# The gMLP's second input half as seven block products over pairs of tiles

## The chip, the core and the metric

The kernel runs on one core of a Trainium2 chip. TensorE (PE) multiplies, VectorE (DVE) and ScalarE (ACT) work elementwise and read the products out of PSUM, GpSimd (POOL) does small and elementwise work in SBUF, and SyncE (SP) issues transfers. Each engine takes its instructions in the order of the program and waits at the first one whose operands are not ready. The metric is the device time of one execution in microseconds (us); the time of a kernel is the median of its runs.

## The reference

Two layers, each a linear attention block A followed by a gated MLP B. The change lies in the second half of `x @ w_in`, which becomes z2:

```
def _B_ref(x, w_in, w_sp, b_sp, w_out):
    z = _gelu(jnp.einsum("bsd,df->bsf", x, w_in))
    z1 = z[..., :Fh]
    z2 = _layernorm(z[..., Fh:], axis=-1)
    g = jnp.einsum("ts,bsf->btf", w_sp, z2) + b_sp[None, :, None]
    return jnp.einsum("bsf,fd->bsd", z1 * g, w_out)

for the two layers:
    x = x + _A_ref(_layernorm(x), A_wqkv, A_wo)
    x = x + _B_ref(_layernorm(x), ...)
```

x is 2048 x 512, `w_in` 512 x 1792 (two halves of 896), `w_sp` 2048 x 2048, all float32.

## The kernel before

The 2048 rows are 16 tiles of 128. A float32 product is three matmuls (`mm3`, lines 115 to 117): both operands are split into a high part h, which ACT copies out (line 101), and a low part l, the rest, which DVE subtracts (line 104), and h·h, h·l and l·h are added up in PSUM. The order of all instructions is written by hand; nothing is reordered later. There are 8 PSUM banks and 22 pages of 128 x 512 in SBUF, handed out oldest first, 4 big tiles (`bigs`) and 6 quads.

A layer has four stages.

- **P1** (`P1.run`, 17 steps) makes keys, values and queries. A step turns a tile (DVE transpose, line 242), splits it, makes K (12 matmuls) and up to step 10 Q (12 more), and adds to the four G banks (12). At the end of a step come side pieces: a weight piece of 128 x 512 is split by ACT and DVE. Fifteen pieces (wv, wo and seven of win2, the second half of `w_in`) are spread over steps 1 to 10: one a step in the first five, two after that.
- **transition** makes the combined matrix W2.
- **P2** (`P2.run`, steps s = 1 to 18) is where the change lies. In step s DVE turns the scaled queries of tile s (`b_high`, transpose, then the high part on ACT), does the denominators of tile s+2 (`a2_den`, lines 556 to 558) and the low part (`b_low`); PE multiplies tile s-1 by W2 (`c`, 12 matmuls); DVE adds it to x (`c2`, line 597) and takes its statistics (lines 178 to 180), POOL makes rs and nb of them (lines 182 to 185), and ACT normalises (`c3`, line 191). `a2_mul` (line 565) and `a` (POOL, line 544) prepare later queries. `d_high` and `d_low` turn and split tile s-2, which came back from DRAM. `e4` normalises z of tile s-4 (ACT, 128 x 896, and for the first eight tiles a subtraction on DVE, line 663). `e` multiplies tile s-3 by win2, two banks of 448 columns with 12 matmuls each, `e2` takes GELU of the banks (line 652), `e3` the statistics of z. Then `f` runs twice: 12 matmuls of 128 x 512 for z1, four tiles at a time, a GELU on ACT (line 677) and a store. f has no work before step 6; seven calls belong to four tiles, so steps 9, 13 and 17 have one call, and five calls are left for the start of P4. The step ends with a piece of win1 (the first half of `w_in`, low part on POOL, line 109) and, from step 8, with `sums.tick`.
- **P4** multiplies by `w_sp`, itself as seven block products of 8 steps each (24 or 18 matmuls a step), gates and makes the output. `Sums` makes the four sums of blocks of `w_sp` on POOL (line 772), once, in the first layer, and keeps them in DRAM: 11 ticks lie in P2 and 21 in P4. Weights of P4 are fetched four steps ahead.

In steps 1 to 4 PE turns the queries, and in steps 2 to 5 it turns the tiles of d, so that those lie in PSUM and not in a page.

Of the kernel before, what the change touches and what calls it, by code (L numbers as in the profile page):

```python
# [10 lines left out]
F32 = mybir.dt.float32  # L11
F32R = mybir.dt.float32r
# [41 lines left out]
def mixer_kernel(ctx: ExitStack, tc: tile.TileContext, x_in, wqkv, wo_d, win1_d, win2_d, wsp_d, bsp_d, wout_d,  # L54
# [58 lines left out]
    def mm3(out, a, b, start, stop):  # L113
# [2 lines left out]
        nc.tensor.matmul(out, ah, bl, start=False, stop=False)  # L116
        nc.tensor.matmul(out, al, bh, start=False, stop=stop)  # L117

    class Weight:


# [42 lines left out]
    def w_wo():  # L164
        return Weight(bigs, [P, 4, 512], [wo_d[c * P:(c + 1) * P, :] for c in range(4)])

    def w_in1():
        return Weight(bigs, [P, NF, 4, P], [win1_d[f] for f in range(NF)])

    def w_in2():  # L170
        return Weight(bigs, [P, 4, FH], [win2_d[f] for f in range(NF)])

    def stats(x, n):

# [72 lines left out]
    class P1:  # L247
        def __init__(self, L):
            self.L = L
            self.st = 2 * L  # L250
            self.x, self.ms, self.xT, self.pk, self.kb, self.r, self.xhl = {}, {}, {}, {}, {}, {}, {}
            self.wk, self.wq, self.wv = (w_square(wqkv, 512), w_square(wqkv, 0, True), w_square(wqkv, 1024))
            self.wo, self.win2 = w_wo(), w_in2()
            self.later = deque(range(NT - DEFER, NT))
            self.turn = Turn(f"xt{L}", range(3) if L == 0 else ())
            self.G = None
            self.zacc = None
# [153 lines left out]

        def run(self):
            side = deque()
            for w in (self.wv, self.wo, self.win2):
                side.extend([w] * len(w.pieces))
            side[0].fetch()
            ND = NT - DEFER
            for s in range(1, NT + 2):
                self.loadx(s + 3)
                self.turn.load(s + 1)  # L420
                turned = 2 <= s < NT and s not in self.turn.by_pe
                if turned:
                    self.T_high(s)
                if s == 1:
                    if not self.kb:
                        self.K(0)
                    self.K(1)
                elif 2 < s <= NT:
                    self.K(s - 1)
                self.ln_a(s + 2)  # L430
                if turned:
                    self.T_low(s)
                if s <= NT:
                    self.K_phi(s - 1)
                if s <= ND:
                    self.Q(s - 1)
                if s == NT + 1:
                    self.late()
                if s <= NT:
                    self.xsplit(s - 1)  # L440
                    self.K_split(s - 1)
                if s + 1 < NT and s + 1 in self.turn.by_pe:
                    self.T(s + 1)
                self.ln_b(s + 2)
                if s <= ND:
                    self.Q_phi(s - 1)
                if s >= 2:
                    self.Gmm(s - 2)
                if s == NT + 1:
                    self.late_phi()  # L450
                for _ in range(min(len(side), 1 if s < 6 else 2)):
                    side.popleft().piece()
                for w in list(side)[:1 if s < 5 else 2]:
                    w.fetch()


    def transition(p1, p2):
# [18 lines left out]
        banks.put(zb)  # L476
        p2.a(0)
        p1.late_phi()
        p2.win1.fetch()
        p2.win1.fetch()  # L480
        p2.zeps = small.tile([P, 32], F32, name="zeps", bufs=1)
        nc.vector.tensor_reduce(p2.zeps, p2.zbc.rearrange("p (h d) -> p h d", d=16), axis=mybir.AxisListType.X,
                                op=OP.add)
# [41 lines left out]
    class P2:  # L525
        def __init__(self, p1):
            self.L = L = p1.L
            self.p1 = p1
            self.win1, self.win2 = w_in1(), p1.win2
            self.qturn, self.xturn = Turn(f"qt{L}", range(5), True), Turn(f"yt{L}", range(4))  # L530
            self.qp, self.qT, self.x, self.ms, self.xB, self.z, self.zms = {}, {}, {}, {}, {}, {}, {}
            self.fq = deque()
            self.fnext = []

        def loadx(self, i):
            if i < NT:
# [89 lines left out]
        def d_low(self, i):  # L626
            b, home, h, l = self.dpart
            low(l, b, h)
            home.put(b)
            n, k = divmod(i, 4)  # L630
            if i in self.xB:
                pages.put(self.xB.pop(i))
            if k == 3:
                self.fnext = [(n, f) for f in range(NF)]

        def e(self, i):
            n, k = divmod(i, 4)
            h, l = self.xT[n]
            s = slice(k * P, (k + 1) * P)
            w = self.win2  # L640
            self.eb = []
            for j in range(2):
                b = banks.get([P, HF])
                o = slice(j * HF, (j + 1) * HF)
                for c in range(4):
                    mm3(b, (h[:, c, s], l[:, c, s]), (w.h[:, c, o], w.l[:, c, o]), c == 0, c == 3)
                self.eb.append(b)

        def e2(self, i):
            z = ztag(i, [P, FH], f"z{self.L}")  # L650
            for j, b in enumerate(self.eb):
                nc.scalar.activation(z[:, j * HF:(j + 1) * HF], b, AF.Gelu_apprx_tanh)
                banks.put(b)

        def e3(self, i):
            self.zms[i] = stats(ztile[i], 2)
# [8 lines left out]
        def f(self):  # L665
# [1 line left out]
                return False  # L667
            n, f = self.fq.popleft()
            h, l = self.xT[n]
            w = self.win1  # L670
            b = banks.get(PAGE)
            for c in range(4):
                mm3(b, (w.h[:, f, c, :], w.l[:, f, c, :]), (h[:, c, :], l[:, c, :]), c == 0, c == 3)
            if f == NF - 1:
                quads.put(*self.xT.pop(n))
            t = pages.get(PAGE)
# [4 lines left out]
            pages.put(t)  # L681
            return True

        def run(self, sums):
            w1 = self.win1
            for s in range(1, NT + 3):
                self.loadx(s + 1)
                self.qturn.load(s + 1)
                if s in self.qturn.by_pe:
# [10 lines left out]
                    self.a2(s + 2)  # L700
                    self.p1.late_phi()
                    self.a(s + 3)
                else:
                    if s < NT:
                        self.b_high(s)
# [18 lines left out]
                    if s <= NT + 1 and not late:  # L724
                        self.d_high(s - 2)
                        self.d_low(s - 2)
                if s >= 4:
                    self.e4(s - 4)
                self.xturn.load(s - 1)
                if s >= 3:  # L730
                    self.e(s - 3)
                    self.e2(s - 3)
                    self.e3(s - 3)
                self.f()
                self.f()
                self.fq.extend(self.fnext)
                self.fnext = []
                w1.piece(True)
                w1.fetch()
                if s > 7:  # L740
                    sums.tick()
                if s >= NT + 1:
                    self.p4.fetch(s - NT - 1)
            self.e4(NT - 1)
            self.win2.free()


    class Sums:
# [2 lines left out]

        def __init__(self):
            self.s = {(m, k): dram.tile([P, 2, 512], F32, name=f"s{m}_{k}") for m in range(1, 5) for k in range(HT)}
            self.todo = deque((k, j, h) for k in range(HT) for j in range(2) for h in range(2))
            self.ahead = deque(self.todo)
            self.raw, self.made, self.done = {}, [], []

        def fetch(self):
            if self.ahead:
                k, j, h = self.ahead.popleft()  # L760
                at = ((j, k), (j, k + HT), (2 + j, k)) if h == 0 else ((2 + j, k + HT),)
                self.raw.setdefault((k, j), []).extend(load(wsp_d[n, s]) for n, s in at)

        def store(self):

            for m, k, j, t in self.made:
                nc.sync.dma_start(self.s[m, k][:, j, :], t)
            pages.put(*self.done)
            self.made, self.done = [], []

# [4 lines left out]
        def tick(self):  # L775
# [4 lines left out]
                self.fetch()  # L780
            self.fetch()
            k, j, h = self.todo.popleft()
            if h == 0:
                a21, a22, a11 = self.raw[k, j][:3]
                self.add(1, k, j, a22, a21, a22)
                self.add(3, k, j, a21, a21, a11)
                self.done = [a21]
            else:
                _, a22, a11, a12 = self.raw.pop((k, j))
                self.add(2, k, j, a11, a22, a11)  # L790
                self.add(4, k, j, a12, a11, a12)
                self.done = [a22, a11, a12]


    class P4:
# [16 lines left out]
        def fetch(self, g):  # L812
# [5 lines left out]
                n, s = {"P1": (2, k), "P2": (2, k + HT), "P4": (0, k + HT)}[p]  # L818
                nc.sync.dma_start(t, wsp_d[n:n + 2, s].rearrange("j p t -> p j t"))
            else:  # L820
                nc.sync.dma_start(t, self.sums.s[{"P6": 2, "P7": 3, "P5": 1, "P3": 4}[p], k])
            self.raw[g] = t

        def operand(self, g):
# [174 lines left out]
        def run(self, nxt):  # L999
# [1 line left out]
            self.prepare(0, 0)  # L1001
            self.fetch(2)
            while p2.f():
                pass
            p2.win1.free()
            self.prepare(1, 1)
            self.fetch(3)
            self.prepare(None, 2)
            self.gb = [bigs.get([P, NF, 512]) for _ in range(NCHK)]
            n = len(self.steps)  # L1010
            for g in range(n):
# [1 line left out]
                self.prepare(g + 2, g + 3)  # L1013
                self.mm(g)
                self.fetch(g + 4)
                if g in (1, 4, 7) or 8 <= g < 28:
                    self.sums.tick()
                if g == 3:
                    self.loadb()
# [44 lines left out]
    for L in range(2):  # L1064
# [3 lines left out]
        p2.loadx(1)  # L1068
        transition(p1, p2)
        p2.p4 = p4 = P4(p2, sums)  # L1070
        p2.run(sums)
        nxt = P1(1) if L == 0 else None
        p4.run(nxt)
        p1 = nxt
# [31 lines left out]
```

## Time and profile before

| | |
|---|---|
| median of three runs | 1394.43 us (1394.32 to 1394.86) |
| profiled execution, its time and its span | 1395.31 us, 1393.5 us |
| granted TensorE clock | 1.0 |
| P2, a step of 13 us in layer 1 (929 to 942): PE, DVE, ACT, POOL busy | 13.00, 8.45, 5.34, 3.81 us |
| the same in layer 0 (239 to 252) | 13.00, 10.96, 4.82, 7.09 us |
| DMA over the span | 162 GB/s; the highest of 40 slices 298 GB/s |
| queues in use | SP's alone; POOL issues no transfer |

Busy times of PE are modelled and overlap from one matmul to the next, so that its rate is read from the starts of its matmuls. The other engines' busy times are those of their instructions.

### The profile page before, as it was taken

The numbers are of one execution on the slowest core, as the hardware profiler recorded it, in microseconds if no ns is written. First come the engines' busy times: TensorE is split into PE (matmuls) and PEld (weight loads), VectorE is DVE, ScalarE is ACT, GpSimd is POOL, SyncE is SP. The second block draws the span as 40 slices with busy tenths as digits, with TensorE's granted clock in tenths as the row PEclk, the third lists the DMA queues.
The fourth block names the chain that finished last, engine by engine and source line by source line (L and its number), as shares of the span: only waits on it lengthen the run. The fifth ranks groups of instructions, "written<-read, shape, count | busy, mean of one in ns | idle before, by whom it ended". The sixth has DMA issues, their size and how long they took to land.

```text
span 1393.5 us, 17586 instructions
## 1 busy us (share of the span) xinstructions
PE 1387.4 (100%) x6270; PEld 1164.0 (84%) x6270; DVE 879.5 (63%) x1251; ACT 582.1 (42%) x899; POOL 416.9 (30%) x502
## 2 busy tenths in 40 slices
PE   9999999999999999999999999999999999999998
PEld 7888888888888888888888888888888888888887
DVE  6775777853755587664567767876426445776642
ACT  6674543444432234241366655444333432342410
POOL 3343344543135541431023424432100000223310
PEclk9999999999999999999999999999999999999999
DMA  5542256776679964354645314555334323544542
GB/s 176 168 131 59 90 166 218 259 226 217 215 235 295 298 228 136 121 203 159 211 129 176 111 46 121 174 176 175 104 122 142 101 96 129 168 134 156 169 143 91
DMA packets 142457, 225.70 MB, mean 162 GB/s; under 512 B 11937, under 2 KB 50593, under 8 KB 142369
## 3 DMA queue, kind: packets, MB, share of 16 engines
q1 hardware_dynamic: 142368, 224.57, 50.1%
q8 instruction: 49, 0.80, 0.3%
q14 instruction: 40, 0.32, 0.1%
HBM read 156.63 MB, written 67.90 MB: 161 GB/s over the span
## 4 chain that ended last, share of the span: by engine, by line
PE 98%; DVE 1%; DMA 0%; POOL 0%; ACT 0%; issue 0%; SPq 0%; POOLq 0%; ACTq 0%
PE bank L117 19%; PE bank L116 19%; PE bank L115 19%; PE bank L897 13%; PE bank L898 13%; PE bank L899 13%; PE bank L203 1%; PE bank L390 0%; DMA pg<-in_wsp_dram 0%; POOL pg L772 0%; ACT z_z L191 0%; DVE st L178 0%; ACT qd L101 0%; POOL rs L183 0%; DVE den L557 0%
## 5 line engine op out<-in xcount | busy, mean ns | idle before, releaser
L898 PE MATMUL bank<-qd,pg 128*128 128x512 f32 x800 | 311.4, 389 | 0.0
L897 PE MATMUL bank<-qd,pg 128*128 128x512 f32 x800 | 311.4, 389 | 0.0
L899 PE MATMUL bank<-qd,pg 128*128 128x512 f32 x800 | 311.4, 389 | 0.0
L863 DVE TENSOR_TENSOR qd<-qd,qd 128x1024 fp32r<-128x1024 f32 x112 | 157.9, 1410 | 157.2 <-ACT qd L856 154.2
L856 ACT ACTIVATE qd<-qd 128x1024 fp32r<-128x1024 f32 x112 | 118.6, 1059 | 239.1 <-DMA qd<-s 101.7
L899 PEld LDWEIGHTS bank<-qd,pg 128*128 128x128 f32 x800 | 150.2, 188 | 31.4
L897 PEld LDWEIGHTS bank<-qd,pg 128*128 128x128 f32 x800 | 150.1, 188 | 31.2
L898 PEld LDWEIGHTS bank<-qd,pg 128*128 128x128 f32 x800 | 150.2, 188 | 31.0
L919 POOL TENSOR_TENSOR bg<-bg,pg 128x512 f32<-128x512 f32 x56 | 78.9, 1413 | 320.7 <-DMA pg<-z 308.6
L117 PE MATMUL bank<-qd,pg 128*128 128x512 f32 x384 | 149.9, 390 | 0.0
L182 POOL TENSOR_SCALAR rs<-mv 128x1 f32<-128x1 f32 x96 | 38.0, 396 | 355.4 <-DVE mv L180 351.8
L191 ACT ACTIVATE pg<-pg,nb,rs 128x512 f32<-128x512 f32 x63 | 51.0, 810 | 179.0 <-POOL nb L185 172.8
L772 POOL TENSOR_TENSOR pg<-pg,pg 128x512 f32<-128x512 f32 x64 | 93.9, 1467 | 94.4 <-DMA pg<-in_wsp_dram 88.5
L115 PE MATMUL bank<-qd,pg 128*128 128x512 f32 x288 | 112.3, 390 | 0.0
L116 PE MATMUL bank<-qd,pg 128*128 128x512 f32 x288 | 112.3, 390 | 0.0
L115 PE MATMUL bank<-bg,qd 128*128 128x448 f32 x256 | 94.1, 368 | 0.0
L117 PE MATMUL bank<-bg,qd 128*128 128x448 f32 x256 | 93.6, 366 | 0.1
L116 PE MATMUL bank<-bg,qd 128*128 128x448 f32 x256 | 93.7, 366 | 0.0
L117 PE MATMUL bank<-qd,bg 128*128 128x512 f32 x224 | 87.5, 391 | 0.0
L116 PE MATMUL bank<-qd,bg 128*128 128x512 f32 x224 | 87.5, 390 | 0.0
L115 PE MATMUL bank<-qd,bg 128*128 128x512 f32 x224 | 87.3, 390 | 0.0
L116 PE MATMUL bank<-wo,qd 128*128 128x512 f32 x224 | 87.2, 389 | 0.0
(128 smaller groups left out, 2606.9 us busy)
## 6 DMA issues: line engine op xcount, KB each, us to landing
qd<-s SPq DMA_DIRECT2D x64, 512.0 KB, 3.5
qd<-in_wsp_dram SPq DMA_DIRECT2D x48, 512.0 KB, 4.2
pg<-in_wsp_dram SPq DMA_DIRECT2D x64, 256.0 KB, 5.2
s<-pg SPq DMA_DIRECT2D x64, 256.0 KB, 5.0
pg<-x SPq DMA_DIRECT2D x64, 256.0 KB, 3.1
z<-pg SPq DMA_DIRECT2D x56, 256.0 KB, 2.7
pg<-z SPq DMA_DIRECT2D x56, 256.0 KB, 3.9
x<-pg SPq DMA_DIRECT2D x48, 256.0 KB, 2.6
```

Source lines behind the costliest of these rows:

```text
L115: nc.tensor.matmul(out, ah, bh, start=start, stop=False)
L116: nc.tensor.matmul(out, ah, bl, start=False, stop=False)
L117: nc.tensor.matmul(out, al, bh, start=False, stop=stop)
L182: nc.gpsimd.tensor_scalar(rs, mv[:, 1:2], LN_EPS, None, op0=OP.add)
L191: nc.scalar.activation(y, x, AF.Identity, bias=nb, scale=rs)
L772: nc.gpsimd.tensor_tensor(t, a, b, op=OP.add)
L856: nc.scalar.activation(w[:, 0], r, AF.Copy)
L863: nc.vector.tensor_sub(w[:, 1], r, w[:, 0].bitcast(F32))
L897: m(out, h[:, o], w[:, 0, j, :], start=start, stop=False, skip_group_check=True)
L898: m(out, h[:, o], w[:, 1, j, :], start=False, stop=False, skip_group_check=True)
L899: m(out, l[:, o], w[:, 0, j, :], start=False, stop=stop, skip_group_check=True)
L919: nc.gpsimd.tensor_tensor(u, u, z1, op=OP.mult)
```

## The change

The second half of the gMLP's input is made for two tiles at once. With the two tiles' x as rows A11, A12 and A21, A22 (halves of the 512 features) and the weight as blocks Bij of 256 x 448, the four products of blocks become seven: P1 = A11·B11, P2 = A12·B21, P3 = S4·B22, P4 = A22·T4, P5 = S1·T1, P6 = S2·T2, P7 = S3·T3, with S1 = A21+A22, S2 = S1-A11, S3 = A11-A21, S4 = A12-S2. One bank X goes on adding P1, P6, P7 and P4, and is read three times on the way. Each product is 6 matmuls of 448 columns. The block sums are made on DVE at the end of d in odd steps, from step 3 on; where d lies in PSUM, ACT copies it out first (`in_sbuf`).

The parts of win2 (seven forms, h and l) and of win1 (seven pieces, h and l) are made in P1 of layer 0, stored in DRAM by SP (`flush`), and in both layers brought in by transfers that POOL issues: forms in P1 and P2, win1 part by part ahead of f. The sums of `w_sp` all move into P4. The statistics and the normalisation of z lag by a pair, and those of the last four tiles come at the start of P4.

```diff
+    def flush():
+        while stores:
+            d, part = stores.popleft()
+            nc.sync.dma_start(d, part.bitcast(F32))
...
+        def form(self, name):
+            t, h, l = (self.work[:, i, :].rearrange("p (c f) -> p c f", c=2) for i in range(3))
...
+            if name == "T1":
+                nc.vector.tensor_sub(t, B("B12"), B("B11"))
...
+            split(h, l, src)
+            stores.extend(...)
...
+    class Parts:
+        def fetch(self):
+            while self.todo and len(self.have) < self.ahead:
+                parts = [pages.get([P, 4, P], F32R) for _ in range(2)]
+                for t, d in zip(parts, self.todo.popleft()):
+                    nc.gpsimd.dma_start(t, d.rearrange("p (c f) -> p c f", c=4))
+                self.have.append(parts)
...
+        def weights_made(self, s, side, make):
+            todo = {5: ("T1",), 6: ("T2",), 7: ("T4",), 8: ("T3",), 9: ("B11", 1), 10: ("B21", 1), 11: ("B22", 1),
+                    12: (2, 3), 13: (2, 3)}.get(s, ())
...
+            for _ in range(0 if 5 <= s < 14 else min(len(side), 1 if s < 5 else 2)):
+                side.popleft().piece()
...
+        def block_sums(self):
+            a, b = (self.in_sbuf(*r) for r in self.rows)
...
+            nc.vector.tensor_add(S1, A21, A22)
+            nc.vector.tensor_sub(S2, S1, A11)
+            nc.vector.tensor_sub(S3, A11, A21)
+            nc.vector.tensor_sub(S4, A12, S2)
+            pages.put(a, b)
+            self.S = []
+            for r in (s, t):
...
+                split(h, l, r)
...
+        def e_first(self, m):
+            i = 2 * m
+            self.X, y = banks.get([P, HF]), banks.get([P, HF])
+            self.product(self.X, m, "P1", start=True)
+            self.product(y, m, "P2", start=True, stop=True)
...
+            nc.scalar.activation(z[:, self.LO], self.X, AF.Copy)
+            self.add(i, self.LO, y)
+            banks.put(y)
+            self.gelu(i, self.LO)
+
+        def e_second(self, m):
+            i, X = 2 * m, self.X
+            Z = banks.get([P, HF])
+            self.product(X, m, "P6")
+            nc.scalar.activation(ztile[i][:, self.HI], X, AF.Copy)
+            self.product(Z, m, "P5", start=True)
+            pages.put(*self.S[0])
+            self.f()
+            self.product(X, m, "P7")
+            z = ztag(i + 1, [P, FH], f"z{self.L}")
+            nc.scalar.activation(z[:, self.HI], X, AF.Copy)
+            self.add(i + 1, self.HI, Z)
+            self.gelu(i + 1, self.HI)
+            self.f()
+            self.product(X, m, "P4", stop=True)
+            nc.scalar.activation(z[:, self.LO], X, AF.Gelu_apprx_tanh)
+            banks.put(X)
+            self.product(Z, m, "P3", stop=True)
+            self.add(i, self.HI, Z)
+            banks.put(Z)
+            self.gelu(i, self.HI)
...
                     if s <= NT + 1 and not late:
                         self.d_high(s - 2)
                         self.d_low(s - 2)
-                if s >= 4:
-                    self.e4(s - 4)
+                    if s % 2:
+                        self.block_sums()
                 self.xturn.load(s - 1)
-                if s >= 3:
-                    self.e(s - 3)
-                    self.e2(s - 3)
-                    self.e3(s - 3)
-                self.f()
-                self.f()
+                m, second = divmod(s - 3, 2)
+                if s >= 3 and not second:
+                    if m >= 2:
+                        self.e4(2 * m - 4)
+                        self.e4(2 * m - 3)
+                    self.e_first(m)
+                    self.f()
+                    self.f()
+                elif s >= 3:
+                    if m >= 1:
+                        self.e3(2 * m - 2)
+                        self.e3(2 * m - 1)
+                    self.e_second(m)
                 self.fq.extend(self.fnext)
                 self.fnext = []
-                w1.piece(True)
-                w1.fetch()
-                if s > 7:
-                    sums.tick()
+                if s <= 2:
+                    self.forms.fetch(3)
+                if s >= 4:
+                    self.win1.fetch()
...
-                if g in (1, 4, 7) or 8 <= g < 28:
+                if g % 5 in (0, 2, 3) or g >= 26:
                     self.sums.tick()
```

In `Sums` a tick of the first sixteen now loads three pages, makes three sums and stores three; a tick of the last sixteen loads two (one of them a sum that was stored), makes one and stores one.

## The prediction

> **What bounds the kernel now.** I read the shares of the engines first, then the chain that ended last, then PE's own waits.
>
> ```profile
> PE 1387.4 (100%) x6270; PEld 1164.0 (84%) x6270; DVE 879.5 (63%) x1251; ACT 582.1 (42%) x899; POOL 416.9 (30%) x502
> ```
> ```profile
> PE bank L390 <- DVE pg L385: 2.3, 1, 2.3
> ```
>
> PE is the bound: it waits once, 2.3 us at the start. PE's timeline gives its rate: the start of the next matmul minus that of this one.
>
> ```profile
> 936.56 0.39 PE L116 MATMUL bank<-qd,pg 128*128 128x512 f32 x1
> 936.79 0.39 PE L117 MATMUL bank<-qd,pg 128*128 128x512 f32 x1
> 937.02 0.36 PE L115 MATMUL bank<-bg,qd 128*128 128x448 f32 x1
> 937.22 0.37 PE L116 MATMUL bank<-bg,qd 128*128 128x448 f32 x1
> ```
>
> 512 columns cost 0.227 us, 448 cost 0.203 (24 of them run from 247.30 to 252.16 in layer 0). A P2 step is c 2.72 + e 4.87 + two f 5.45 = 13.04 us, and c2 starts 13.05 us apart. What the other engines need is a matter of their order, so next come the timelines of DVE, ACT and POOL in one step of layer 1.
>
> ```profile
> 944.74 1.05 DVE L242 STREAM_TRANSPOSE pg<-pg 128x512 f32<-128x512 f32 x1
> 945.63 0.64 DVE L556 TENSOR_REDUCE den<-pg 128x32 f32<-128x512 f32 x1
> ...
> 948.70 0.69 DVE L104 TENSOR_TENSOR pg<-pg,pg 128x512 fp32r<-128x512 f32 x1 [1.82 <-ACT pg L101]
> 950.27 0.69 DVE L597 TENSOR_TENSOR pg<-pg,bank 128x512 f32<-128x512 f32 x1 [0.88 <-PE bank L117]
> 950.99 0.69 DVE L178 BATCH_NORM_STATS2 st<-pg 128x6 f32<-128x512 f32 x1
> 951.72 0.18 DVE L180 BATCH_NORM_AGGREGATE mv<-st 128x2 f32<-128x6 f32 x1
> ...
> 954.98 0.69 DVE L104 TENSOR_TENSOR qd<-pg,qd 128x512 fp32r<-128x512 f32 x1 [1.50 <-ACT qd L101]
> ```
> ```profile
> 953.61 0.82 ACT L191 ACTIVATE pg<-pg,nb,rs 128x512 f32<-128x512 f32 x1 [4.94 <-POOL nb L185]
> 954.33 0.62 ACT L101 ACTIVATE qd<-pg 128x512 fp32r<-128x512 f32 x1
> 954.85 1.12 ACT L191 ACTIVATE z_z<-z_z,nb,rs 128x896 f32<-128x896 f32 x1
> 955.88 0.52 ACT L652 ACTIVATE z_z<-bank 128x448 f32<-128x448 f32 x1
> ```
>
> From c2 (950.27) to the end of d's low part (955.67) is 5.4 us of waiting in turn: DVE, POOL (aggregate's end 951.90 to ACT's start 953.61: 1.71), ACT, DVE. Today none of it reaches PE: c and e use what was made a step earlier. PE's end to DVE's start is 0.2 us, ACT to DVE 0.04.
>
> **The change, part by part.**
>
> *PE work.* A pair of tiles takes 42 matmuls of 448 in place of 48: 6 x 0.203 = 1.22 us, 16 pairs in the two layers: -19.5 us, if PE never waits.
>
> *The new loop in P2.* PE now depends inside a step on the slow chain. P7 adds to bank X, which ACT must first have copied out, and that copy stands in ACT's queue behind c3's normalise and d's high part, which wait for c of the same step. P6 likewise waits for the copy in `e_first`, which stands behind the block sums' high parts and two e4. And `add`, after P3, is what DVE must end before it goes on to the next step's transpose. I walk one steady pair from P3's end, in us. Odd step: add at 0.2 (0.6: between 0.43 for 256 columns, L104, and 0.68 for 512, L597) to 0.8; transpose 0.9, 1.7; denominators 1.24 (L556 to L558 without contention), 2.94; low part 0.6, 3.55 (c was done at 2.9); c2 0.72, 4.27; statistics 0.91, 5.18; POOL 1.71, 6.89; normalise 0.72, 7.61; d's high part 0.62, 8.23; low part, 8.87; four block sums of 256 columns at 0.42, 10.55; the second sum pair's high part 0.52, 11.1; two e4 at 1.03, 13.17; copy 0.52, 13.7; `add`, 14.35. PE has done c, P1, P2, two f and the next c by 13.3, so P6 waits 0.5. Even step: on ACT three GELUs at 0.5 after that add, then the high part of the queries, 16.66; low part 17.3; c2 18.0; statistics 18.9; POOL 20.6; normalise 21.4; d's high part 21.9; copy 22.4; P7 at 22.6. PE, which has done P6, P5 and one f by 19.0, waits 3.6. Then P7, f, P4, P3: 1.22+2.72+1.22+1.22, end at 29.0. The loop closes on itself, so no slack gathers: a steady pair takes 29.0 us where PE's work is 24.9 and where it took 26.1 (23.4 with one f less, steps 9 and 13, for PE's missing f is off the loop).
>
> All pairs of a layer: steps (7,8) and (11,12) +2.9 each; (9,10) +5.5; (13,14) +5.2 (a little less on ACT); (15,16) -0.4 (no queries in 16); (17,18) +1.7 (no c, but P6 waits for block sums and two e4); (5,6), no f in 5 and two copies out of PSUM (0.55 each) ahead of the sums: 26.6 for 21.2, +5.4; (3,4), no f at all: P6 waits 4.7, P7 4.3, P4 0.9, less 1.2 saved, +8.5. Together +31.7, both layers **+63.4**, PE's saving included. Bounds: 35.6 if only the steps from 7 on stall; 80 if each step loses another 0.5.
>
> *Behind the waits.* PE's queue has f, P4, P3 and the next c behind P7; DVE's next transpose waits for P3, and so c2, POOL and ACT.
>
> *P1 of layer 0.* Fifteen split pieces become four and then, from step 5, forms. The timeline of DVE shows the step full:
>
> ```profile
> 64.60 0.69 DVE L311 SCALAR_TENSOR_TENSOR z_q<-bank,z_q 128x512 f32<-128x512 f32 x1 [1.16 <-ACT z_q L310]
> 65.21 1.28 DVE L104 TENSOR_TENSOR bg<-pg,bg 128x512 fp32r<-128x512 f32 x2
> 66.41 1.07 DVE L242 STREAM_TRANSPOSE pg<-pg 128x512 f32<-128x512 f32 x1
> ...
> 74.45 1.08 DVE L242 STREAM_TRANSPOSE pg<-pg 128x512 f32<-128x512 f32 x1
> ```
>
> 8.04 us from transpose to transpose, PE's step 36 x 0.227 = 8.17. The two lows (1.2) become a subtraction of 896 (1.2), ACT's high part (0.9, waiting for it) and a low part (1.2; L104 on 128x896 is 1.29): +2.1 beyond the slot, 10.1 to 10.2. Late per step: 2.05 x 4 (steps 5 to 8), 0.7 x 2 (9, 10: low 1.2 + piece 0.6), then against 24 x 0.227 = 5.44, where DVE's period was 5.3: 1.7 (11), 1.06 x 4 (12 to 15, two pieces): 15.5. The low part of a turned tile ends about 4.4 before K needs it, so **+11**; bounds 0 and 20. P1 of layer 1 loses seven pieces; PE was full there: 0.
>
> *Transfers by SP.* 14 stores of 0.46 MB and 14 of 0.26 in some ten steps of P1 (slices 4 and 5 show 59 and 90 GB/s) and as part of what DVE makes late; SP's loads for the step stand ahead of them: 0.
>
> *Transfers by POOL.* Up to four of 0.26 MB a P2 step, 1 MB in 14 us; SP and POOL together stay under 250 GB/s. POOL issued none before, so the price of an issue on POOL is bounded by its shortest and longest instruction, 0.10 (L1095) and 1.96 (L917). After an even step's z statistics POOL has 7.7 us until the next c statistics; four issues take 0.4 to 7.8: 0, hidden. Nearest in kind are the short ones. The pages they fill were given back two f before or earlier. The Trainium skill, DMA: Bandwidth & Descriptors, Latency and other measured facts, gives about 1 us to the first byte on this path; four would be 4 us by it, the sum the same; no run shows it yet.
>
> *Sums in P4.* Layer 0's P2 loses 11 ticks (POOL there was no bound). In P4 three ticks in five steps, 9 sums x 1.47 = 13.2 of 27 us on POOL, then one a step. In steps 26 to 31 weights, tick and gate are 1.57 MB in 4.08 us, 385 GB/s against 298 in the fullest slice: some 7 us late, against four steps (16 us) of fetch ahead: 0, bound 10. Late statistics of z hide under the five f left over.
>
> The sum: 1395.3 + 63.4 + 11 = 1469.7 for the profiled execution, which lies 0.9 over the median: **1469 us**.
>
> **The rivals.**
> *PE covers it all.* P5 and f behind P6, two f behind P2, are enough; the end is then 1395.3 - 19.5 - 0.9 = 1375. For it: PE waits nowhere today, DVE has 4.6 of 13 us free. Against: the walk's loop is made of measured pieces in program order. It decides below 24.9 us a pair, that is if 4 us of 29 are not there. 0.12, of which 0.01 for waits that just eat the saving up.
>
> *POOL's issues hold up the statistics.* At 2.5 us each, four take 10 in the even step's 7.7: +2.3 for 7 pairs in two layers, +32: 1501. 0.08.
>
> *PE's clock falls in the waits.* The first ten warm-up matmuls took 4.63 us, 0.46 each, twice the rate later: (0.463-0.227) x 10 = 2.4 us lost per cooling. Eight waits per layer are of 3.4 to 4.7 us: 16 x 2.4 = +38, 1507. For it: those starts; against: nothing in this trace after 2.3 us shows an idle PE. 0.08. The Trainium skill, TensorE: Matmul & The Clock Gate, The HAM clock gate, has the clock halve after an idle window of some 3.4 us that runs freely; my waits would be at its edge, and it speaks for a few of these, not for all.
>
> **How the numbers follow.** My forecast 0.72, its own range 1430 (early steps and P1 absorbed: 1394.4 + 35.6) to 1494 (P1 20, P4 10, P2 some 6 a layer more). The clock and POOL cases reach 1507, so 1430 to 1507 leaves out 1375 and the tails. A difference under 0.2% (2.8 us) can't be told from none. Faster 0.11, same 0.01, slower 0.88.
>
> **What would show it.** PE waits on ACT's copies of the bank (before P7, 3 to 4 us, 16 times; before P6), all inside P2; PE's 448-column matmuls 672 for 768; P2 pairs 29 us apart by c2; waits in P1 of layer 0 from step 7; POOL idle before the statistics. I am wrong if c2 of a pair stays under 26 us, if the waits lie on POOL or on a transfer, or if P4 waits.

## The result

The changed kernel takes 1517.9 us (median of four runs, 1517.1 to 1521.3) against 1394.4 in the same comparison: a ratio of 1.089, 95% interval 1.0871 to 1.0909. It is slower, as forecast, but by 123 us where 75 were forecast (1469), and outside the range (1430 to 1507).

The shares of the engines and the granted clock of the profiled execution after (span 1515.3 us):

```profile
PE 1420.2 (94%) x6174; PEld 1169.8 (77%) x6174; DVE 962.5 (64%) x1399; ACT 633.9 (42%) x973; POOL 483.8 (32%) x628
PEclk9999989989999999999999998999899999999999
```

PE has 96 matmuls less and its busy time is 33 us longer. The row of the granted clock (in tenths; 9, the highest digit, is 90% or more) has four eights where the kernel before has nines throughout, and the mean clock over the span is 0.967 (1.0 before). What PE waits for (total, times, longest, in us):

```profile
PE bank L828 <- ACT z_z L857: 39.3, 12, 6.5
PE bank L828 <- ACT z_z L848: 27.1, 10, 3.0
PE bank L115 <- ACT z_h L101: 6.2, 4, 2.6
PE bank L1139 <- ACT qd L1098: 4.0, 2, 2.0
```

L828 is the first matmul of a block product; L857 and L848 are ACT's copies of bank X that P7 and P6 wait for. PE's timeline at one of them, P7 in step 8 of layer 1 (start, duration, engine, line):

```profile
998.66 0.74 PE L828 MATMUL bank<-bg 128*128 128x448 f32 x1 [6.51 <-ACT z_z L857]
999.20 0.57 PE L829 MATMUL bank<-bg,bg 128*128 128x448 f32 x1
999.57 0.57 PE L830 MATMUL bank<-bg,bg 128*128 128x448 f32 x1
...
1002.52 0.39 PE L116 MATMUL bank<-qd,pg 128*128 128x512 f32 x1
1002.75 0.39 PE L117 MATMUL bank<-qd,pg 128*128 128x512 f32 x1
```

Two losses stand in these rows. PE waits 6.51 us; then its matmuls start 0.37 us apart instead of 0.20 for 448 columns (0.43 instead of 0.23 for 512), until 3.6 us later they are at full rate again. The view of windows (bounds, length, busy time of PE, PEld, DVE, ACT and POOL, granted clock, DMA) has the clock at 0.50 from the middle of the wait to that point:

```profile
995.38:1002.21 6.83, 3.55 (x9) 3.10 (x10) 4.83 (x10) 2.79 (x5) 4.02 (x9) 0.50 0.49 159
```

DVE's and ACT's timelines before it:

```profile
986.77 0.61 DVE L840 TENSOR_TENSOR z_z<-z_z,bank 128x448 f32<-128x448 f32 x1
990.86 1.09 DVE L356 STREAM_TRANSPOSE pg<-pg 128x512 f32<-128x512 f32 x1 [3.48 <-issue]
993.50 0.68 DVE L744 TENSOR_TENSOR pg<-pg,bank 128x512 f32<-128x512 f32 x1
```
```profile
996.85 0.81 ACT L305 ACTIVATE pg<-pg,nb,rs 128x512 f32<-128x512 f32 x1 [4.23 <-POOL nb L299]
997.56 0.61 ACT L101 ACTIVATE qd<-pg 128x512 fp32r<-128x512 f32 x1
998.08 0.52 ACT L857 ACTIVATE z_z<-bank 128x448 f32<-128x448 f32 x1
```

This is the walk of the forecast, link by link: transpose, c2 (L744), statistics, POOL's nb, normalise (L305), d's high part, and only then the copy for P7. One link was not in it: the transpose starts 3.48 us late, waiting for nothing that the view names.

PE's starts split the time (work: matmuls at the full rate; cold: what slower starts add; waits: the rest; 2.2 us of the first stage after and 4.2 of the last are in none of the three):

```
                 before            after                        longer by
                 length   length   work   cold  waits
P1, layer 0       147.8    164.2   142.5   6.9   12.6              16.4
P2, layer 0       203.9    247.0   193.0  16.6   37.3              43.1
P4, P1 layer 1    486.3    498.3   486.2   4.1    8.1              12.0
P2, layer 1       203.4    248.9   193.2  15.8   39.9              45.5
P4, layer 1       352.1    356.9   347.8   1.9    3.0               4.8
all              1393.5   1515.3  1362.6  45.4  100.9             121.8
```

Before, cold and waits were 2.0 and 2.4 us. So the change saves its 20 us of work, adds 98 us of waits (94 in the forecast: 83 in P2 and 11 in P1) and 43 us of cold matmuls (0 in the forecast). Up to the kernel's last microseconds the granted clock is at 0.50 in 19 stretches, 99 us in all, with PE busy in 82 of them: an estimate of 82 x (1 - 0.23/0.43) = 38 us for the clock's part of the 43. The other 5 are starts a little late at full clock.

### The profile page after: what moved, and what is told of

The parts are those of the page before. It is cut to its first block, busy times and chain, and to the rows that moved or that the text cites. A ratio compares the mean times of both kernels' runs of the same rounds, so it can differ in the third digit from the quotient of the medians.

```text
span 1515.3 us, 18123 instructions
## 1 busy us (share of the span) xinstructions
PE 1420.2 (94%) x6174; PEld 1169.8 (77%) x6174; DVE 962.5 (64%) x1399; ACT 633.9 (42%) x973; POOL 483.8 (32%) x628
## 5 line engine op out<-in xcount | busy, mean ns | idle before, releaser
L1139 PE MATMUL bank<-qd,pg 128*128 128x512 f32 x800 | 313.3, 392 | 7.2 <-ACT qd L1098 4.0
L1140 PE MATMUL bank<-qd,pg 128*128 128x512 f32 x800 | 313.5, 392 | 3.0 <-DVE qd L1105 3.0
L1141 PE MATMUL bank<-qd,pg 128*128 128x512 f32 x800 | 312.9, 391 | 0.0
L1105 DVE TENSOR_TENSOR qd<-qd,qd 128x1024 fp32r<-128x1024 f32 x112 | 166.0, 1482 | 132.3 <-ACT qd L1098 131.3
L117 PE MATMUL bank<-qd,pg 128*128 128x512 f32 x608 | 241.7, 398 | 1.6 <-DVE pg L104 1.4
L115 PE MATMUL bank<-qd,pg 128*128 128x512 f32 x512 | 203.4, 397 | 3.4 <-ACT pg L101 3.1
L116 PE MATMUL bank<-qd,pg 128*128 128x512 f32 x512 | 202.4, 395 | 0.0
L1139 PEld LDWEIGHTS bank<-qd,pg 128*128 128x128 f32 x800 | 151.1, 189 | 40.1 <-ACT qd L1098 4.9
L1140 PEld LDWEIGHTS bank<-qd,pg 128*128 128x128 f32 x800 | 151.3, 189 | 35.5 <-DVE qd L1105 4.1
L1141 PEld LDWEIGHTS bank<-qd,pg 128*128 128x128 f32 x800 | 151.3, 189 | 31.5
L117 PEld LDWEIGHTS bank<-qd,pg 128*128 128x128 f32 x608 | 116.4, 192 | 32.0 <-DVE pg L104 7.4
L1013 POOL TENSOR_TENSOR pg<-pg,pg 128x512 f32<-128x512 f32 x64 | 98.1, 1535 | 96.8 <-DMA pg<-in_wsp_dram 58.7
L115 PEld LDWEIGHTS bank<-qd,pg 128*128 128x128 f32 x512 | 98.4, 192 | 24.9 <-ACT pg L101 5.6
L116 PEld LDWEIGHTS bank<-qd,pg 128*128 128x128 f32 x512 | 98.1, 192 | 19.8 <-DVE qd L104 0.3
L305 ACT ACTIVATE pg<-pg,nb,rs 128x512 f32<-128x512 f32 x63 | 51.0, 810 | 144.8 <-POOL nb L299 135.2
L101 ACT ACTIVATE pg<-pg 128x512 fp32r<-128x512 f32 (+1 forms) x93 | 57.3, 617 | 88.3 <-DVE pg L356 56.0
L356 DVE STREAM_TRANSPOSE pg<-pg 128x512 f32<-128x512 f32 x75 | 81.4, 1086 | 16.7 <-DMA z<-pg 9.8
L115 PE MATMUL bank<-wo,qd 128*128 128x512 f32 x224 | 87.1, 389 | 0.0
L116 PE MATMUL bank<-wo,qd 128*128 128x512 f32 x224 | 87.1, 389 | 0.0
```

What stands on the lines that cost most here:

```text
L101: nc.scalar.activation(h, src, AF.Copy)
L115: nc.tensor.matmul(out, ah, bh, start=start, stop=False)
L356: nc.vector.transpose(y.rearrange("p c (t m) -> p m c t", m=4), r.rearrange("p (m c j) -> p m c j", m=4, c=4))
L1013: nc.gpsimd.tensor_tensor(t, a, b, op=OP.add)
L1105: nc.vector.tensor_sub(w[:, 1], r, w[:, 0].bitcast(F32))
L1139: m(out, h[:, o], w[:, 0, j, :], start=start, stop=False, skip_group_check=True)
```

## The experiments

Theory A: the loop of copies and the page that delays the transpose make the waits, and PE is cold because it has waited. Rivals: the clock falls with the change's load; one link alone holds the loop; GpSimd's issues hold it. Medians in us, ratio to the kernel before with its interval, and cold and waits from each profiled execution:

```
             median   ratio, 95% interval       waits  cold
after        1517.9   1.0890 (1.0871, 1.0909)   100.9  45.4
warm         1531.2   1.0980 (1.0964, 1.0997)    79.4  32.7   46.5 us more work
e4late       1518.9   1.0887 (1.0871, 1.0904)   108.9  36.7
p6early      1495.5   1.0728 (1.0712, 1.0744)    85.7  38.4
pagelate     1513.6   1.0849 (1.0831, 1.0867)   100.2  46.4
idlez        1503.9   1.0781 (1.0765, 1.0797)    88.0  45.7
loopshort    1499.6   1.0747 (1.0722, 1.0772)    87.9  34.9
looppage     1538.1   1.1032 (1.1014, 1.1051)   118.4  47.4
idlezloop    1517.2   1.0877 (1.0861, 1.0893)   101.8  45.7
making       1509.5   1.0819 (1.0803, 1.0835)    97.1  38.1
finishearly  1521.3   1.0906 (1.0890, 1.0922)   103.6  45.4
finishmid    1509.0   1.0820 (1.0802, 1.0838)    95.7  40.1
best         1496.7   1.0735 (1.0717, 1.0753)    88.3  34.0
bestfetch    1486.5   1.0662 (1.0639, 1.0684)    80.0  37.3
```

### Is PE cold because it waits?

**pauses** puts waits into the kernel before, which has none of the change. `pause` stands ahead of c, in layer 1 also behind it.

```diff
+        def pause(self, k):
+            if k:
+                b = banks.get([P, P])
+                nc.tensor.matmul(b, ones, ones, start=True, stop=True)
+                for _ in range(k):
+                    nc.gpsimd.tensor_tensor(ones, ones_f, ones_f, op=OP.mult)
+                nc.tensor.matmul(b, ones, ones, start=True, stop=True)
+                banks.put(b)
```

> The kernel before, unchanged but for pauses of PE in P2: two small matmuls over the tile of ones with k GpSimd operations between them, which rewrite that tile. Layer 0: one pause in each of steps 5 to 15, k from 1 to 10. Layer 1: two pauses of equal k, 12 matmuls of c between them, k from 1 to 6. It has no products by blocks and none of the change's transfers. Theory A (the matmuls are cold because PE has waited, wherever the wait is from): behind waits from about 2.5 us on, and behind two shorter ones close together, matmuls of 448 columns start 0.37 us apart instead of 0.20 for 3.4 us or more; below 1.5 us, alone, none are cold. Theory B (the clock falls with the change's own load, its transfers or GpSimd): every matmul at 0.20 us whatever the pause; the time is 1394.8 plus the pauses. Theory C (no wait below 3.4 us counts): cold matmuls only behind single waits over 3.4 us, none in layer 1's pairs.

1581.9 us. Two pauses in PE's timeline of layer 1, one of 1.49 and one of 2.30 us:

```profile
1041.11 0.33 PE L661 MATMUL bank<-ones 128*128 128x128 f32 x1 [1.49 <-POOL ones L660]
1041.27 0.45 PE L115 MATMUL bank<-qd,pg 128*128 128x512 f32 x1
1041.56 0.40 PE L116 MATMUL bank<-qd,pg 128*128 128x512 f32 x1
1041.79 0.39 PE L117 MATMUL bank<-qd,pg 128*128 128x512 f32 x1
...
1073.40 0.33 PE L661 MATMUL bank<-ones 128*128 128x128 f32 x1 [2.30 <-POOL ones L660]
...
1075.17 0.63 PE L115 MATMUL bank<-qd,pg 128*128 128x512 f32 x1
1075.59 0.63 PE L116 MATMUL bank<-qd,pg 128*128 128x512 f32 x1
1076.02 0.63 PE L117 MATMUL bank<-qd,pg 128*128 128x512 f32 x1
```

After 1.49 us the next matmuls are soon 0.23 apart; after 2.30 us they turn cold 1.4 us later and stay so for 2.9 us, up to the next pause. Over all 33 pauses (120.8 us): of the 8 up to 1.55 us none left cold matmuls; of the 25 from 2.30 us on 24 did (one of 2.77 did not). Each cost 1.3 to 2.8 us more, 46.2 in all, 1.9 on average, and a pause of 9.48 cost no more than one of 2.97. (Pauses and cold matmuls make 167 of the 187 us by which this kernel is longer; the rest are the pauses' own small matmuls and the starts around them.) Outside P2 this kernel's cold and waits are as before. So waits alone make PE cold, as theory A says, but its two shorter pauses in a row (1.49 and 1.55) cooled nothing; the last section shows what decides. Theory B falls: the kernel has none of the change's transfers. Theory C falls: nine pauses between 2.30 and 3.25 us cooled.

**warm** fills the wait ahead of P7 with 14 matmuls into a spare bank, which nothing reads.

```diff
+            warm = banks.get([P, HF])
+            wl = self.forms.get("T1")[0]
+            for _ in range(14):
+                nc.tensor.matmul(warm, ones, wl[:, 0, :], start=True, stop=True)
+            banks.put(warm)
             self.product(X, m, "P7")
```

> The changed kernel with 14 idle matmuls of 448 columns ahead of P7 in every pair, into a bank of their own: 14 x 0.203 = 2.8 us of PE work where PE waited 3.6 to 6.5 us for ACT's copy. Theory A (a wait of over some 3.4 us halves PE's clock for the next 3.4 us, and that is what the walk of the prediction left out: 52 of the 122 us): the gaps shrink below the point where the clock falls, PE's granted clock in P2 rises from 0.92 to 0.97 or more and the time falls by 20 to 40 us, to 1480-1498. Theory B (the slow matmuls lie inside waits and cost nothing, the loop alone sets the time): no change within 5 us, or a few us more where the idle matmuls are longer than the wait.

1531.2: the expected gain was missed. The clock rose to 0.981, cold matmuls fell by 13 us and waits by 21, but the dummies are 46.5 us of work. They stand in PE's queue at a fixed length, where the waits vary up to 6.5 us, so they probably stretch the loop that they should fill; that is argued, not shown. The run shows that fewer waits go with fewer cold matmuls; what a wait costs is shown by pauses.

### Which link holds the loop?

**e4late** puts the normalisations of the pair before behind `e_first`, **p6early** puts P6 and its copy (`e_six`) right behind c, **loopshort** does both.

```diff
-                    if m >= 2:
-                        self.e4(2 * m - 4)
-                        self.e4(2 * m - 3)
                     self.e_first(m)
+                    if m >= 2:
+                        self.e4(2 * m - 4)
+                        self.e4(2 * m - 3)
```
```diff
                     if s <= NT:
                         self.c(s - 1)
+                    if s % 2 == 0:
+                        self.e_six((s - 3) // 2)
+                    if s <= NT:
                         self.c2(s - 1)
```

> The changed kernel with the two e4 of an odd step behind the copy, the addition and the GELU of the first half instead of ahead of them. Theory A (a closed loop through ACT, DVE, POOL and PE sets a pair's length, and the two e4, 1.03 us each on ACT, are a link of it): 2.1 us less in each pair from step 7 on, 6 pairs in two layers, 25 us, a little more with fewer cold matmuls: 1485-1495. Theory B (DVE's and ACT's sum of work, or pages, bound the pair): within 5 us of the changed kernel, since no work goes away.

> The changed kernel with P6 and the copy of bank X after it put right behind c in even steps, ahead of c2, the normalise and the turned tile of d on DVE and ACT; from step 6 on. Theory A (the loop): P7 no longer waits for anything made from c of its own step, the loop loses c2 to d's high part (about 5 us a pair and the cold matmuls behind its wait), so that a pair falls from 28-34 us to some 25-27: 45 to 65 us less, 1455-1475, and the wait of P7 for ACT's copy all but gone after step 5. Theory B (throughput of DVE and ACT, or pages): under 15 us less.

> P6 and its copy right behind c, and the normalisations of the pair before behind e_first, together. Theory A (a pair's period is the longer of two branches, ScalarE's copies between the products and the page of f's GELU that the transposes reuse; the normalisations' order matters only where the page doesn't): 1485 to 1495, hardly better than with P6 alone (1495.5). Theory B (the normalisations on ScalarE ahead of e_first's copy are the remaining link): 1460 to 1475.

e4late gains nothing where 25 us were expected (+1.0, within its runs' spread). p6early gains 22, half of the least that was expected; loopshort gives 1499.6, no better than p6early alone and 5 above theory A's range, and theory B's 1460 to 1475 falls. In e4late the view names what the transpose waits for:

```profile
989.63 1.08 DVE L356 STREAM_TRANSPOSE pg<-pg 128x512 f32<-128x512 f32 x1 [2.09 <-DMA z<-pg]
```

It is the store of z1 (z<-pg): the page that the transpose writes was just given back by f, whose store is still under way.

**pagelate** gives f's page back one f later; **idlez** takes no page for f's GELU at all, but the slot of a z tile that lies idle between the queries' use and z's.

```diff
-            t = pages.get(PAGE)
+            k = self.idle_z.popleft() if self.idle_z else None
+            t = pages.get(PAGE) if k is None else main.tile(PAGE, F32, tag=f"z{k}", bufs=1, ...)
...
+                self.idle_z = deque(k for k in (s + 1, s - 1) if k < NT)
```

> The changed kernel with the page of f's GELU given back one f later. The transpose of the queries in steps 8 and 12 sat idle for 3.4 us, and its output page is the one that f's GELU had filled in the step before and whose store to DRAM was still under way. Theory A (that page is what it waited for, and it is in the loop): some 3 us less in two pairs of each layer, 10 to 16 us in all with the clock: 1502-1508. Theory B (it waited for its own input, the tile loaded back): no change within 3 us.

> As the changed kernel, but f's GELU writes into the slot of a z tile that lies idle for four steps, so f's stores hold no page. Theory A (two branches: the copies' loop rules, the page second): the wait of the transposes for a page goes, the copies' link stays: 1505 to 1515, P7 still waits some 3 us a pair. Theory B (the page is what holds the loop): 1470 to 1490.

pagelate gains 4 where 10 to 16 were expected; the transpose starts at once, and the next to take a page waits instead, the low part:

```profile
989.57 1.10 DVE L356 STREAM_TRANSPOSE pg<-pg 128x512 f32<-128x512 f32 x1
...
993.75 0.69 DVE L104 TENSOR_TENSOR pg<-pg,pg 128x512 fp32r<-128x512 f32 x1 [2.00 <-DMA z<-pg]
```

idlez gains 14 (1503.9, a little more than theory A expected) and its waits before P7 are at most 3.1 us. The page is a branch of its own, beside the copies. Its cold matmuls are not fewer (45.7 us against 45.4): waits cut from 6.5 to 3.1 us still cool.

**looppage** is loopshort with two pages freed (one piece of f's weights less ahead), f's page given back one f later, and the statistics of a pair behind its products; **idlezloop** has idlez's slots instead of the freed pages and the late page.

> As loopshort, and two pages more (one chunk less of in1's parts ahead), f's page given back one f later, and the statistics of a pair behind its products. Theory A: the 2 us per pair of waiting for a page go with the copies' link, about 20 us of waits and 8 us of cold matmuls below P6 alone: 1462 to 1478. Theory B (the page is hidden by the copies): within 5 us of loopshort. In every run the sum of waits and of cold matmuls should fall together, cold about 0.4 us for each us of waits.

> f's GELU into an idle z tile, P6 and its copy right behind c, the normalisations of the pair before behind e_first, the statistics behind e_second: looppage without the lack of f's weights. Theory A (both branches shortened): the steady pair, 31 us before and 28.7 in looppage with 2.6 us of waiting for weights, falls to 26 to 27: 1455 to 1475. Theory B (a third branch has the same length): 1485 to 1500.

Both missed theory A's numbers. In looppage the pairs are 28.7 us apart by c2, and the waits on the copies of X are under 24 us in all, but PE waits 58.6 us in 14 places, up to 10 us, for f's weights. idlezloop, with the same place for the statistics but the third piece ahead, waits 14.7 us for them, so most of the 58.6 come from the two pages: they were not spare. In idlezloop two waits of 7 us for weights remain (next part), and P6 waits 31.4 us in 10 places for the copy ahead of it, against 13.5 in loopshort. Why is not shown.

### P1, P4's start, and GpSimd's queue

**making** lets GpSimd make the differences one step earlier and the low parts of win1, instead of DVE.

```diff
+            if 4 <= s < 8:
+                make.difference(("T1", "T2", "T4", "T3")[s - 4])
...
-            split(h, l, r)
+            split(h, l, r, True)
```

> In P1 of layer 0 the differences of weight blocks are made by GpSimd one step earlier, and the low parts of the in1 weights by GpSimd too, instead of VectorE. Theory A (VectorE's added work in these steps makes PE wait, 10 us of waits and 6 us of cold matmuls by the trace): P1 of layer 0 keeps 2 to 8 of its 16.4 us: 1503 to 1510. Theory B (PE waits for the weights' transfers or for GpSimd, which carries more now): 1516 to 1530.

1509.5, 8.4 less, as theory A expected: P1 of layer 0 is 9 us shorter, nearly half of them cold matmuls. **finishearly** and **finishmid** move the last four tiles' normalisations, which P4's first products need, ahead of the five f left over, or behind the second of them.

> The normalisations left over from P2's last four tiles are emitted ahead of P2's last products over f instead of behind them. Theory A (P4's first products wait because ScalarE and VectorE come to these normalisations only after the GELUs of f): the waits at P4's start, 4.3 us in layer 0 and 2.8 us in layer 1, go, and with them the cold matmuls behind them (2 to 4 us): 1507 to 1512. Theory B (they wait for the operands' own chain of copy, subtraction and transfer): 1516 to 1520, and the waits stand where they were.

> The changed kernel with the last normalisations behind the second of the five products of f that P4 begins with, when GpSimd has issued the last transfers of f's weights. Theory A (P4's first waits, 4.3 us in layer 0 and 2.8 us in layer 1, come from these normalisations' place behind f's GELUs; finishearly only traded them for f's weights, whose transfers stood on GpSimd behind the statistics): both waits gone, f's 3.86 us waits too: 1507 to 1513. Theory B (the place doesn't matter): 1516 to 1521.

finishearly gains nothing (+3.4), finishmid 8.9 us. P4's first waits are gone in both. The difference is GpSimd's queue. In finishearly:

```profile
405.97 0.23 POOL L296 TENSOR_SCALAR rs<-mv 128x1 f32<-128x1 f32 x1 [11.92 <-DVE mv L294]
...
409.18 2.23 POOL L250 DMA_DIRECT2D pg<-win  x4
```
```profile
412.38 0.79 PE L115 MATMUL bank<-qd,pg 128*128 128x512 f32 x1 [3.86 <-DMA pg<-win]
```

The transfers of f's weights stand behind statistics that wait for DVE, and f pays 3.86 us. finishmid puts the statistics where no transfer is left.

**best** joins idlezloop, making and finishmid; **bestfetch** also issues f's transfers ahead of the pair's statistics.

```diff
                     self.e_second(m)
+                    if s >= 4:
+                        self.win1.fetch()
                     if m >= 1:
                         self.e3(2 * m - 2)
                         self.e3(2 * m - 1)
```

> As idlezloop, with the differences of P1 of layer 0 made as in the run making, and with the last normalisations behind the second of f's products over the last group, when no transfer of weights is left behind them on GpSimd. Theory A: idlezloop less 8 us (measured in making) less 4 to 8 us (P4's first waits of 4.3 and 2.8 us and the cold matmuls behind them): 1440 to 1462, still above the kernel before, since steps 3 to 6 have no work over f to fill their waits. Theory B (the savings hide one another): within 5 us of idlezloop.

> As best, with f's transfers issued on GpSimd ahead of the statistics of a pair instead of behind them. Theory A (in best the two waits of 6.9 us for f's weights come from eight transfers queued behind those statistics): both waits go, 14 us of waits and some 5 us of cold matmuls: 1474 to 1484. Theory B (they come from pages that are not yet free): 1492 to 1500.

best takes 1496.7, 35 above the range's upper end, which was reckoned from idlezloop's forecast, itself missed by 42. One part of it has the same reason as above, eight transfers behind the statistics:

```profile
385.54 4.34 POOL L245 DMA_DIRECT2D pg<-win  x8 [0.17 <-issue]
```
```profile
388.46 0.80 PE L115 MATMUL bank<-qd,pg 128*128 128x512 f32 x1 [6.86 <-DMA pg<-win]
```

bestfetch takes 1486.5, 2.5 above its range: those waits fall from 14.0 to 5.3 us, not to none. So the transfers' place explains some 10 of the 35 us; where the other 25 come from is not shown. It is the fastest variant found, 6.6% slower than the kernel before: its steady pair still takes 28.7 to 29.6 us, and PE still waits 52 us on ACT's copies of X.

## Why the forecast was wrong

**The step that failed** is the price of P2's waits: "Together +31.7, both layers +63.4, PE's saving included" lets a wait cost its own length. In pauses, 24 of 25 waits of 2.30 us and more cost 1.9 us again, on average, in matmuls at half rate; the changed kernel's cold matmuls are 43 us, where the sum had nothing. This was the rival "PE's clock falls in the waits", held at 0.08. That its +38 comes near the 43 is in part luck, for its sum is another: 2.4 us for 16 waits of 3.4 us and more, where the trace has 19 stretches at half rate and only four waits over 3.4 us (15 of the waits that it names are of 2.3 to 3.4). The evidence against it, "nothing in this trace after 2.3 us shows an idle PE", was no evidence: a kernel whose PE never waits can't show what a wait does. Once the walk gave 3 us waits in every pair, the clock belonged in the sum. The Trainium skill, TensorE: Matmul & The Clock Gate, HAM oscillation — how this bites in real kernels, states the abstract rule as no idle gaps of PE over some 3.4 us; taken as a threshold it was misleading here, since pauses of 2.30 to 3.25 us cooled PE too. The mechanism on that page, a kernel that cools in every round of its loop, is what this one does in seven of the eight pairs of each layer.

**P2's walk** held in the order of its links, which is the one in the rows above. That its sum held too, 77 us of waits in the two P2 against 83, is luck. In the pairs of steps (7,8) and (11,12) PE waits 6.2 to 6.5 us, all of it ahead of P7, where 4.1 were forecast (2.9 longer and 1.2 of saved work), because the transpose came late for a page; in the other pairs up to step 14 it waits 3.6 to 6.5 us where 6.4 to 9.9 were. In idlez, without the wait for the page, some 64 us are left. By c2 the pairs (7,8) and (11,12) are 33.5 to 34.3 us, (9,10) and (13,14) 27.6 to 29.9, with cold matmuls, against 28.6 to 29.0 forecast. (The forecast's first pair adds up to +8.7, not +8.5.)

**"The pages they fill were given back two f before or earlier"** was wrong in kind: it looked at the pages that the transfers fill, and not at who takes the next page. The transposes did, and waited 2 to 3.5 us for f's store; worth 14 us (idlez).

**P1 of layer 0, +11:** 10.4 us more waits, as said, and 6 us of cold matmuls: +16.4.

**P4, taken as 0 with "Late statistics of z hide under the five f left over":** wrong. ACT comes to those normalisations after the five GELUs, and P4's first products wait 4.3 and 2.8 us. That is the forecast's own sign of being wrong, "if P4 waits". The stages that hold P4 are 16.8 us longer in all, 8.9 of which finishmid removes. One wait of 3.2 us in layer 0 lies where the sums now run, for which the forecast had a bound of 10; that the sums cause it is not shown.

**POOL's issues, 0:** held in this kernel; four take 2.24 us, 0.56 each:

```profile
983.83 2.24 POOL L250 DMA_DIRECT2D pg<-win  x4 [2.61 <-DVE pg L801]
```

The rival that they hold up the statistics falls. The forecast's upper price of an issue, 1.96 us, was the mean of a group and not its longest instruction, which takes 2.28: four would have been 9.1 us, more than the 7.7 it had to hide them in. The reverse, statistics holding up the issues, is what three variants ran into.

The sum with what was measured: 1395.3 - 20 (work) + 98 (waits) + 43 (cold) = 1516, against 1517.1 of the profiled execution.

## What to carry over

When a change makes PE wait where it never did, price each wait of more than about 2 us at its length plus what PE loses while it is cold (here 1.9 us), and add up waits that fall within some 3.4 us (last section); saving 20 us of matmuls is worth nothing if it closes a loop over three other engines. Look at who takes the page that was just given back, and at what stands in front of a transfer in the queue that issues it: an early place in the program can be a late one there. Shortening one link of such a loop mostly shows the next: here copies, pages, GpSimd's queue, and the copies again.

## What was not expected of the hardware

What decides is not the length of one wait but how long PE is idle within fixed stretches of time. In all sixteen traces the granted clock is recorded as 1.0 or 0.50, and every stretch at 0.50 lasts 3.41 us or a multiple of it, except where the kernel ends. All of them lie on one grid of 3.41 us per execution. In pauses, the pause of 2.77 us that cooled nothing runs from 1114.61 to 1117.38, and the next, of 2.97 us, which cooled, from 1120.58 to 1123.55. The view of windows along the grid:

```profile
1112.36:1115.78 3.42, 2.25 (x11) 1.67 (x9) 0.35 (x2) 1.21 (x3) 0.93 (x3) 1.00 0.20 77
1115.78:1119.19 3.41, 1.81 (x8) 1.54 (x9) 0.81 (x1) 0.00 (x0) 1.39 (x3) 1.00 0.66 231
1119.19:1122.61 3.42, 1.39 (x7) 0.94 (x5) 1.99 (x4) 0.00 (x0) 1.65 (x4) 1.00 0.02 5
1122.61:1126.02 3.41, 2.47 (x7) 2.25 (x8) 1.15 (x2) 1.17 (x2) 1.86 (x5) 0.50 0.47 154
```

The first pause is split between two windows, in which PE is still busy for 2.25 and 1.81 us. The second leaves PE busy for 1.39 us of one window, and the window behind it has the clock at 0.50. Counted over the sixteen traces (from 20 us on), all 218 windows at full clock with PE busy for less than 1.4 us are followed by one at 0.50, and none of the 6233 with 1.8 us or more; between the two, 44 of 87 are. This view ends a matmul some 0.16 us after the next can start. Reckoned from the starts, with 0.227 and 0.203 us of work for 512 and 448 columns, the bound is sharper: no window with less than 1.97 us of idle PE was followed by one at 0.50, every one with more than 2.10 us was, and in between 17 of 36.

A wait of 1.80 us can thus be enough. In bestfetch PE waits 0.76 and, six microseconds later, 1.80 us (977.05 to 978.85), and 1.5 us after that its matmuls start 0.37 apart.

```profile
978.85 0.47 PE L826 MATMUL bank<-bg,qd 128*128 128x448 f32 x1 [1.80 <-ACT z_z L865]
979.16 0.37 PE L827 MATMUL bank<-bg,qd 128*128 128x448 f32 x1
...
980.38 0.57 PE L827 MATMUL bank<-bg,bg 128*128 128x448 f32 x1
980.75 0.57 PE L828 MATMUL bank<-bg,bg 128*128 128x448 f32 x1
981.12 0.57 PE L826 MATMUL bank<-bg 128*128 128x448 f32 x1
```
```profile
976.95:980.36 3.41, 1.61 (x8) 1.42 (x8) 1.31 (x2) 2.73 (x6) 2.58 (x5) 1.00 0.76 221
980.36:983.78 3.42, 3.42 (x10) 2.90 (x10) 1.30 (x3) 1.20 (x3) 0.43 (x1) 0.50 1.05 313
```

The wait lies wholly in one window; the earlier 0.76 us lies two windows before, with a fully busy one between. The slow rate begins with the next window, up to 1.4 us after the wait has ended and with PE busy again. What decides in the narrow band between 1.97 and 2.10 us stays open.
